# Twelve rounds of ordering by latest times in a kernel's own instruction scheduler, with new durations, a shared VectorE/GpSimd port, and other places for the last block's weight tiles

## Chip, cores and metric

The kernel runs on 1 core of one Trainium2 chip. The metric is the device time of one execution in microseconds (us). Three runs of the kernel before took 1750.62, 1752.32 and 1753.2 us; the median, 1752.32 us, is the number to beat.

## What is computed

Three stages follow each other on 4608 tokens of 512 features, all in float32:

```python
def reference(q, k, v, w_gate, w_val, w_out, w_in, w_out2):
    # attention inside chunks of 64 tokens: batch 8, heads 8, sequence 576, head size 64
    s = (q_c @ k_c.T) / 8;  a = exp(s - max(s));  a = a / (sum(a) + 1e-9)
    x = (a @ v_c)                      # 4608 x 512
    # layer 1: inner size 1536
    g = x @ w_gate
    x = (g * sigmoid(g) * (x @ w_val)) @ w_out
    # layer 2: inner size 2048
    h = x @ w_in
    return (h * sigmoid(1.702 * h)) @ w_out2
```

## The kernel before

**Tiling.** Attention works on units of 128 tokens (36 of them, `attend`, L464). Both layers work on blocks of 512 tokens (nine blocks). The weights of layer 1 are taken in two passes of six slices of the inner size, those of layer 2 in two passes of eight: passes 0 and 1 are layer 1, passes 2 and 3 are layer 2. Attention for a block is done inside pass 0, one block ahead of its use; block 0's attention has nothing to hide behind. A pass runs over all nine blocks, and in each block over its groups (three in layer 1, two in layer 2). Partial results of passes 0 and 2 go to DRAM and are added in passes 1 and 3.

**A group.** Each group multiplies two 2x2 block matrices by seven products in place of eight (`product`, L568; the inputs of the seven come from sums made beforehand, `token_combos` for the tokens and `combos` for the weights). Every float32 operand is split into a high and a low part (`split`, L244: ScalarE casts the high part, VectorE or GpSimd subtracts it from the source for the low part), and `mm3` (L248) issues three matmuls for each pair, on L249, L250 and L251. A product is 12 matmuls of 128x256 into one PSUM bank. What follows a product reads its bank: a ScalarE copy, or a VectorE addition. In layer 1 the products take turns between two banks (`ga` and `gb`, or `s` and `a`). In layer 2 all products of a group go to the one bank `ga`, some of them on top of the sum that is there (`group_gated`, L631), so a product may start only when what followed the last one has read the bank.

**Second multiplication.** Layer 1 has `second` (L622, three matmuls of 128x512 into `ya` or `yb`, here called a Y piece). Layer 2 has `last_product` (L715, six matmuls of 128x256 into `ya`, `yb`, `gb`, `s` or `a`, here a filler, since it stands between products). These pieces wait in a list, `pend`, and are taken between the products of the next group. A group of layer 2 has 7 products and 14 fillers.

**Weights.** They come from the host in packed form and are converted on the way in (`conv_part`, L323: two ScalarE and two VectorE instructions for 128x512), in pass 0 right before use for that pass, later as jobs spread over the pass before. Tiles live in rings of SBUF places: ring `w` has 21 places, ring `o` has 3. In pass 3 the first group's second weights stay in `w` for all blocks; the second group's are loaded anew in each block into the three places of `o` (in `fn` inside the main loop). A load into a place waits until the fillers that read the earlier tile are through.

**Order.** The kernel lists about six thousand operations with an engine, a duration in us, a due time (`prio`), reads and writes (`Program.op`, L76). `emit` (L99) then walks forward in time: on the engine that can start first it takes, among the operations that could start within 0.3 us (0.1 us on VectorE) of the earliest, the one with the lowest `prio`, and issues it. Durations are formulas such as `act_us`, `dve_us` and `pool_us` (L213 to L219). When data goes from another engine to TensorE, the planner allows `late` extra time: 1.2 us, or `near` where an operation names it, 1.0 us for most of layer 2 (`prog.slack`, L904). Every engine, and the DMA queue of SyncE, runs its list in the order in which it was issued, so an instruction that waits holds up all that stand behind it on its engine. 24 single matmuls with priority 9999 (L824) fill TensorE before the first product.

**End.** `o_sum` (L733) adds up the output quarters in pass 3: for the last two quarters GpSimd adds three times in a row (`yv`, `t`, `t`) to tiles loaded from DRAM, VectorE adds the last bank, and SyncE stores.

Of the kernel before, what the change touches and what calls it, by code (L numbers as in the profile page):

```python
# [9 lines left out]
F32R = mybir.dt.float32r  # L10
# [3 lines left out]
ALU = mybir.AluOpType  # L14
# [12 lines left out]
class Buf:  # L27
# [3 lines left out]
    def __init__(self, make, prev=None, before=None, whole=None):  # L31
        self.make, self.prev, self.before, self.whole = make, prev, before, whole
        self.users, self.writers, self.tile = [], [], None
# [18 lines left out]
class Ring:  # L52
    def __init__(self, pool, tag, bufs):
# [12 lines left out]
class Op:  # L66
    __slots__ = ("eng", "us", "fn", "prio", "deps", "follows", "table", "near", "n", "done_at")


class Program:  # L70


    def __init__(self):
        self.ops, self.slack = [], None

    def op(self, eng, us, fn, reads=(), writes=(), prio=0, table=None, near=None):  # L76
        o = Op()
        o.eng, o.us, o.fn, o.prio, o.table, o.near, o.n = eng, us, fn, prio, table, self.slack if near is None and eng not in ('pe', 'dma') else near, len(self.ops)
# [20 lines left out]
    def emit(self):  # L99
        waiting = {o: len(o.deps) + len(o.follows) for o in self.ops}  # L100
        after = {}
        for o in self.ops:
            for d in (*o.deps, *o.follows):
                after.setdefault(d, []).append(o)
        ready = {}
        for o in self.ops:
            o.done_at = 0.0
            if not waiting[o]:
                ready.setdefault(o.eng, []).append(o)
        free, table = {}, None  # L110
        left = len(self.ops)
        while left:
            pick = None
            for eng, todo in ready.items():
                if not todo:
                    continue
                t = free.get(eng, 0.0)
                start = [max(t, o.done_at) for o in todo]
                first = min(start)
# [5 lines left out]
            free[o.eng] = s + o.us + (1.3 if o.table and o.table != table else 0.0)  # L125
            end = free[o.eng] + (2.0 if o.eng == "dma" else 0.0)
            table = o.table or table
            o.fn()
            left -= 1
            for a in after.get(o, ()):  # L130
                if o in a.deps:
# [3 lines left out]
                    a.done_at = max(a.done_at, end + ((0.0 if a.eng == "pe" else 0.13) if a.eng == o.eng else late))  # L135
                waiting[a] -= 1
                if not waiting[a]:
                    ready.setdefault(a.eng, []).append(a)
# [3 lines left out]
def attention_two_moe_kernel(ctx: ExitStack, tc: tile.TileContext, q, k, v, wg, wv, wo, wi, wo2, out):  # L142
# [45 lines left out]
    for name, space in (("const", None), ("sb", None), ("ps", PSUM), ("dram", DRAM)):  # L188
# [5 lines left out]
    ring.update({tag: Ring(pool["ps"], tag, 1) for tag in ("ya", "yb", "ga", "gb", "s", "a")})  # L194
# [36 lines left out]
    def copy(dst, src, n, prio, eng="act", cut=lambda ap: ap, near=None):  # L231
        if eng == "act":
            op("act", act_us(n), lambda: nc.scalar.copy(out=dst.ap, in_=cut(src.ap)), [src], [dst], prio, near=near)  # L233
        elif eng == "pool":
            op("pool", pool_us(0.6 * n), lambda: nc.gpsimd.tensor_copy(dst.ap, cut(src.ap)), [src], [dst], prio)  # L235
        else:
            op("dve", dve_us(n), lambda: nc.vector.tensor_copy(dst.ap, cut(src.ap)), [src], [dst], prio)
# [39 lines left out]
    GV, YS, OS = 1.42, 0.70, 0.714  # L277
# [45 lines left out]
    def conv_part(raw, t, n, prio):  # L323
# [4 lines left out]
        op("act", act_us(n), lambda: nc.scalar.activation(  # L328
            out=t.ap, in_=raw.ap[:, :, 2], func=AF.Relu, scale=up, bias=offset.ap[:, :1]), [raw, offset], [t], prio)
        op("act", act_us(n), lambda: nc.scalar.activation(  # L330
            out=word(1).bitcast(F32), in_=raw.ap[:, :, 2], func=AF.Relu, scale=up, bias=offset.ap[:, 1:]),
           [raw, offset, t], [raw], prio)
        op("dve", dve_us(1.3 * n), lambda: nc.vector.scalar_tensor_tensor(
            out=t.ap.bitcast(I32), in0=t.ap, scalar=-4096 * up, in1=word(1).bitcast(F32), op0=ALU.add, op1=ALU.min),
           [raw, t], [t], prio)
        op("dve", dve_us(1.4 * n), lambda: nc.vector.scalar_tensor_tensor(
# [127 lines left out]
    def attend(u, prio, load_prio, bufs=None, both=None):  # L464
# [20 lines left out]
        op("pe", 1.2, lambda: blocks(s.ap, qb.ap, kb.ap), [qb, kb], [s], prio)  # L485
        m = ring["m"].new([P, H, 1])
        z = ring["z"].new([P, H, 1])
        op("dve", 0.69, lambda: nc.vector.tensor_reduce(out=m.ap, in_=heads(s.ap), axis=AX.X, op=ALU.max), [s], [m], prio)
        op("dve", 0.71, lambda: nc.vector.tensor_tensor(
            out=heads(e.ap), in0=heads(s.ap), in1=m.ap.to_broadcast([P, H, CH]), op=ALU.subtract), [s, m], [e], prio)  # L490
        op("act", act_us(512), lambda: nc.scalar.activation(out=e.ap, in_=e.ap, func=AF.Exp, scale=scale), [e], [e], prio, "exp")
        op("dve", 0.69, lambda: nc.vector.tensor_reduce(out=z.ap, in_=heads(e.ap), axis=AX.X, op=ALU.add), [e], [z], prio)
        op("dve", 0.24, lambda: nc.vector.tensor_scalar(out=z.ap, in0=z.ap, scalar1=1e-9, scalar2=None, op0=ALU.add),
           [z], [z], prio)
        op("dve", 0.2, lambda: nc.vector.reciprocal(out=z.ap, in_=z.ap), [z], [z], prio)
        op("dve", 0.71, lambda: nc.vector.tensor_tensor(
# [12 lines left out]
        op("pe", 0.75, transposes, [e, ident], [pt], prio)  # L509
        op("act", 0.59, lambda: nc.scalar.copy(out=e.ap, in_=pt.ap), [pt], [e], prio)  # L510
        o = ps() if both is None else pt
        op("pe", 1.2, lambda: blocks(o.ap, vb.ap, e.ap), [vb, e], [o], prio)
# [353 lines left out]
    for p, (layer, gs) in enumerate(passes):  # L866
        jobs = spread(p)
        for b in range(NB):
            t = start[p][b]
            xs = X.pop((p, b))  # L870
            for j, g in enumerate(gs):
# [31 lines left out]
                else:  # L903
                    prog.slack = 1.0  # L904
# [88 lines left out]
```

## Time and profile before

| what | value |
|---|---|
| median of three runs | 1752.32 us (1750.62 to 1753.2) |
| the profiled execution's own time | 1753.21 us |
| its span, first to last instruction | 1751.4 us |
| mean granted TensorE clock | 0.987 |
| TensorE matmul busy | 1704.3 us, 97% |
| VectorE, ScalarE, GpSimd busy | 1111.5, 882.3, 735.2 us |
| DMA traffic | 477.91 MB, 273 GB/s |

The profiled execution took 1.8 us more than its span. A matmul in a stream is followed by the next one well before its own shown duration ends, so busy time on TensorE overstates how full it is; what tells is the time from one matmul's start to the next one's. Waits that are listed for PE are those of a matmul, those for PEld of the weight load ahead of it.

### The profile page before, as it was taken

Reading aid. Unit: us, or ns where it says so; the run is one execution under the profiler, and the core shown is the slowest. Engines: PE = TensorE matmul, PEld = TensorE weight load, DVE = VectorE, ACT = ScalarE, POOL = GpSimd, SP = SyncE. Lnnn points to the kernel's source line nnn. Section 1 sums busy time; section 2 is a strip of 40 time slices with the busy share of each in tenths; the row PEclk is TensorE's granted clock in tenths of the full one; section 3 lists DMA queues with packets and bytes.
Section 4 is the critical chain, followed back from the end, with each engine's and each line's share of the span. In section 5 each row is a group of like instructions: output and inputs, shape, how many; then the busy total and the mean of one; then the engine's idle time right before and its main releaser. Section 6 shows DMA issues by size and latency. Waiting matters only on the chain.

```text
span 1751.4 us, 36463 instructions
## 1 busy us (share of the span) xinstructions
PE 1704.3 (97%) x14392; PEld 1617.2 (92%) x14392; DVE 1111.5 (63%) x1632; ACT 882.3 (50%) x1535; POOL 735.2 (42%) x762
## 2 busy tenths in 40 slices
PE   6889999999999999999999999999999999999998
PEld 6779989889999999999999989999999999999997
DVE  6887678767774464544445548778775555555555
ACT  5776666666763343333333446555544444444442
POOL 4665464636652145212222235656662133333333
PEclk8989999999999999999999999999999999999999
DMA  6568888887869988777778998989989977777774
GB/s 246 188 230 279 289 293 280 270 270 276 295 229 366 331 290 292 260 251 246 254 258 281 352 353 279 320 288 312 310 299 321 364 248 227 218 233 232 228 223 137
DMA packets 187323, 477.91 MB, mean 273 GB/s; under 512 B 20112, under 2 KB 47760, under 8 KB 187152
## 3 DMA queue, kind: packets, MB, share of 16 engines
q1 hardware_dynamic: 187152, 475.58, 80.5%
q8 instruction: 114, 1.87, 0.4%
q14 instruction: 57, 0.47, 0.1%
HBM read 334.46 MB, written 141.03 MB: 271 GB/s over the span
## 4 chain that ended last, share of the span: by engine, by line
PE 86%; DVE 5%; ACT 2%; issue 2%; DMA 1%; POOL 0%; POOLq 0%; ACTq 0%; DVEq 0%
PE ga L249 11%; PE ga L251 10%; PE ga L250 10%; PE yb L249 4%; PE ya L250 4%; PE ya L249 4%; PE ya L251 4%; PE yb L251 4%; PE yb L250 4%; PE gb L249 4%; PE gb L251 4%; PE gb L250 4%; PE s L249 2%; PE s L251 2%; PE s L250 2%
## 5 line engine op out<-in xcount | busy, mean ns | idle before, releaser
L249 PE MATMUL ga<-x,w 128*128 128x256 f32 x1640 | 472.9, 288 | 10.9 <-ACT u L233 3.9
L250 PE MATMUL ga<-x,w 128*128 128x256 f32 x1640 | 463.9, 283 | 3.0 <-DVE x L242 3.0
L251 PE MATMUL ga<-x,w 128*128 128x256 f32 x1640 | 464.6, 283 | 0.4 <-POOL w L242 0.4
L249 PEld LDWEIGHTS ga<-x,w 128*128 128x128 f32 x1640 | 311.7, 190 | 26.7 <-ACT u L233 9.8
L250 PEld LDWEIGHTS ga<-x,w 128*128 128x128 f32 x1640 | 311.6, 190 | 8.2 <-DVE x L242 3.3
L251 PEld LDWEIGHTS ga<-x,w 128*128 128x128 f32 x1640 | 311.5, 190 | 0.6 <-POOL w L242 0.6
L233 ACT COPY u<-ga 128x512 f32<-128x512 f32 x231 | 135.3, 586 | 254.3 <-PE ga L251 252.1
L242 DVE TENSOR_TENSOR c<-u,ga 128x512 f32<-128x512 f32 x143 | 98.2, 687 | 239.1 <-PE ga L251 229.7
L653 ACT ACTIVATE xr<-c 128x512 f32<-128x512 f32 x140 | 88.3, 631 | 135.1 <-DVE c L242 128.2
L242 DVE TENSOR_TENSOR c<-u,gb 128x512 f32<-128x512 f32 x125 | 85.4, 683 | 95.7 <-ACT u L233 68.0
L249 PE MATMUL gb<-x,w 128*128 128x256 f32 x500 | 143.4, 287 | 1.5 <-DVE c L242 1.5
L251 PE MATMUL gb<-x,w 128*128 128x256 f32 x500 | 141.8, 284 | 0.0
L250 PE MATMUL gb<-x,w 128*128 128x256 f32 x500 | 141.6, 283 | 0.0
L613 ACT ACTIVATE h<-c 128x512 f32<-128x512 f32 x108 | 67.9, 632 | 118.6 <-DVE c L242 118.0
L235 POOL CAST ws<-t 128x256 fp32r<-128x256 f32 x78 | 41.0, 526 | 193.7 <-DMA wd_b<-ws 85.5
L242 DVE TENSOR_TENSOR xr<-xr 128x512 f32<-128x512 f32 x140 | 117.4, 839 | 5.4 <-ACT xr L653 3.1
L242 POOL TENSOR_TENSOR k<-xr,q 128x512 fp32r<-128x512 f32 x24 | 37.5, 1564 | 173.8 <-ACT q L233 64.7
L242 DVE TENSOR_TENSOR hl<-h,hh 128x512 fp32r<-128x512 f32 x108 | 92.0, 872 | 17.0 <-ACT hh L233 16.8
L249 PEld LDWEIGHTS gb<-x,w 128*128 128x128 f32 x500 | 95.4, 191 | 4.3 <-DVE c L242 1.7
L242 POOL TENSOR_TENSOR u<-u 128x512 f32<-128x512 f32 x36 | 48.7, 1352 | 117.7 <-ACT u L233 117.7
L242 POOL TENSOR_TENSOR yv<-yv,e 128x512 f32<-128x512 f32 x18 | 23.2, 1288 | 177.2 <-ACT e L233 115.9
L250 PEld LDWEIGHTS gb<-x,w 128*128 128x128 f32 x500 | 95.5, 191 | 2.0
(253 smaller groups left out, 5077.0 us busy)
## 6 DMA issues: line engine op xcount, KB each, us to landing
x<-x_dram SPq DMA_DIRECT2D x189, 512.0 KB, 5.3
o<-od_b SPq DMA_DIRECT2D x126, 512.0 KB, 4.7
o<-od_a SPq DMA_DIRECT2D x102, 512.0 KB, 5.3
x_dram<-x SPq DMA_DIRECT2D x63, 512.0 KB, 4.3
wd_b<-ws SPq DMA_DIRECT2D x56, 256.0 KB, 5.0
od_b<-ws SPq DMA_DIRECT2D x56, 256.0 KB, 5.1
w<-wd_b SPq DMA_DIRECT2D x28, 512.0 KB, 6.2
raw<-in_moe_w_out SPq DMA_DIRECT2D x56, 255.8 KB, 4.8
```

The source lines that it names most:

```text
L233: op("act", act_us(n), lambda: nc.scalar.copy(out=dst.ap, in_=cut(src.ap)), [src], [dst], prio, near=near)
L235: op("pool", pool_us(0.6 * n), lambda: nc.gpsimd.tensor_copy(dst.ap, cut(src.ap)), [src], [dst], prio)
L242: lambda: e.tensor_tensor(out=dst.ap, in0=of_a(a.ap), in1=of_b(b.ap), op=by), [a, b], [dst], prio, near=near)
L249: nc.tensor.matmul(o, ah, bh, start=first, stop=False, **kind)
L250: nc.tensor.matmul(o, ah, bl, start=False, stop=False, **kind)
L251: nc.tensor.matmul(o, al, bh, start=False, stop=last, **kind)
L613: op("act", act_us(512), lambda h=h, i=i: nc.scalar.activation(out=h.ap, in_=of(0)(c[i].ap), func=AF.Silu), [c[i]], [h], prio, "silu")
L653: op("act", act_us(512), lambda: nc.scalar.activation(out=h.ap, in_=c.ap, func=AF.Gelu_apprx_sigmoid), [c], [h], prio, "gelu")
```

## The change

The change touches the planner, the durations that it is given, and one ring.

- `order` takes the place of the forward walk of `emit`. It picks by `key` in place of `prio`, with a window and a start time for each engine. Operations of GpSimd and those of VectorE that read no PSUM bank (and aren't exempt by `port=False`) share a port: the second one of two starts to work when the port is free. The switch of ScalarE's function table costs 1.28 us. A DMA costs 0.47 us of issue, and transfers stand in line at 0.865 of their nominal time. From TensorE to another engine 0.32 us are allowed (`HOP`), and 0.5 us on top (`SLACK`), or `near`, where TensorE waits for another engine.
- `dues` walks backward from the end and gives each operation its latest time. `replay` runs the list in order without slack, with a TensorE clock of two levels, and returns the end. `emit` does this twelve times, each time with keys halfway between the old key and the latest time, and issues the list with the earliest end.
- The durations are new, conversions have their own (`conv_us`), and `prog.slack = 1.0` is gone.
- In the last block of the last pass the second group's weight tiles take places of ring `w` in place of ring `o`.

The diff, cut to its core:

```diff
@@ class Ring
+        b.bank = self.pool is self.banks
@@ class Program
-        self.ops, self.slack = [], None
+    HOP = {("pe", "dve"): 0.32, ("pe", "act"): 0.32, ("pe", "dma"): 0.3}
+    WINDOW = {"pe": 0.3, "dve": 0.1, "act": 0.3, "pool": 0.3, "dma": 0.0}
+    FREE = {"pe": 1.3, "pool": 0.7, "dma": 0.7, "act": 0.0, "dve": 0.0}
+    SLACK = 0.5
+    LOAD = 1.28
+    ROUNDS = 12
...
+        o.port = eng == "pool" or eng == "dve" and port is not False and not any(a.bank for b in reads for a in b.line())
@@ def emit -> hop, order, dues, replay, emit
-                s, o = min(((s, o) for s, o in zip(start, todo) if s <= first + (0.1 if eng == "dve" else 0.3)), key=lambda x: (x[1].prio, x[1].n))
...
-                    late = (0.3, 1.2)[a.eng == "pe" and o.eng != "pe"] + (1.5 if o.eng == "dma" else 0.0)
-                    if a.near is not None and o.eng != "dma":
-                        late = a.near
+    def hop(self, d, o):
+        return 0.0 if d.eng == o.eng else self.HOP.get((d.eng, o.eng), 0.06)
+    def order(self):
...
+                t = free[eng]
+                limit = min(max(t, o.ready) for o in todo) + self.WINDOW[eng]
+                o = min((o for o in todo if o.ready <= limit), key=lambda o: (o.key, o.n))
+                s = max(t, o.ready)
...
+            if o.eng == "dma":
+                free["dma"] = s + 0.47
+                moved = max(s + 1.5, moved) + 0.865 * o.us
+                o.end = moved + 1.3
+            else:
+                if o.table and o.table != table:
+                    s, table = s + self.LOAD, o.table
+                if o.port:
+                    o.end = max(s + 0.1, port) + o.us - 0.1
+                    port = o.end - 0.1
+                else:
+                    o.end = s + o.us
+                free[o.eng] = o.end - (0.05 if o.eng != "pe" else 0.0)
...
+                    late = self.hop(o, a)
+                    if a.eng == "pe" != o.eng:
+                        late += self.SLACK if a.near is None else a.near
+                    a.ready = max(a.ready, o.end + late)
...
+    def dues(self, seq):
...
+                    t = min(t, a.due - self.hop(o, a) - (self.SLACK if a.eng == "pe" != o.eng else 0.0))
...
+            elif o.eng == "pe":
+                o.due = free = min(t, free) - o.us
+            else:
+                o.due = t - o.us
...
+    def replay(self, seq):
...
+                s = max([free[eng], *(d.end + self.hop(d, o) for d in o.deps)])
...
+    def emit(self):
...
+        for i in range(self.ROUNDS):
+            seq = self.order()
+            self.dues(seq)
+            last = self.replay(seq)
+            if best is None or last < best[0]:
+                best = last, seq
+            for o in self.ops:
+                if o.prio < 9999:
+                    o.key = (o.key + o.due) / 2
+        for o in best[1]:
             o.fn()
@@ durations (others likewise: matmul pieces, softmax steps, GV, YS, OS)
-        return (200 + n) / 1.2e3
+        return 0.23 + n / 1.385e3
+    def conv_us(n):
+        return 0.30 + n / 1.113e3
-        return (148 + n) / 0.96e3
+        return 0.15 + n / 0.966e3
-        return (128 + n) / 0.46e3
+        return 0.18 + n / 0.465e3
@@ main loop, layer 2
-                    prog.slack = 1.0
...
-                                        w = ws[n] = ring["o"].new([P, 2, 2, 256], F32R)
+                                        tag = "w" if (p, b) == (NPASS - 1, NB - 1) else "o"
+                                        w = ws[n] = ring[tag].new([P, 2, 2, 256], F32R)
```

Two places on TensorE, one on VectorE and one on the DMA queue show how instructions move. Line numbers of the change are about 119 higher.

**TensorE, a stretch of pass 3 in the steady state**, from the last matmul of one product (`ga<-x,w`) over the filler (`yb<-w,...`; `w` holds its weights, `hh` and `hl` the high and low part) to the first matmul of the next product. Before:

```order
L251 MATMUL ga<-x,w 128x256
L249 MATMUL yb<-o,h 128x256
L250 MATMUL yb<-o,h 128x256
L251 MATMUL yb<-o,h 128x256
L249 MATMUL yb<-o,h 128x256
L250 MATMUL yb<-o,h 128x256
L251 MATMUL yb<-o,h 128x256
L249 MATMUL ga<-x,w 128x256
```

And in the changed kernel, from the second of the filler matmuls that follow a product to the first matmul of the next:

```order
L369 MATMUL yb<-w,hh 128x256
L370 MATMUL yb<-w,hl 128x256
L368 MATMUL yb<-w,hh 128x256
L369 MATMUL yb<-w,hh 128x256
L370 MATMUL yb<-w,hl 128x256
L368 MATMUL yb<-w,hh 128x256
L369 MATMUL yb<-w,hh 128x256
L370 MATMUL yb<-w,hl 128x256
L368 MATMUL yb<-w,hh 128x256
L369 MATMUL yb<-w,hh 128x256
L370 MATMUL yb<-w,hl 128x256
L368 MATMUL ga<-x,w 128x256
```

Before, six filler matmuls stand between these two products; now twelve. In all of layer 2, six filler matmuls alone stand between two products 32 times before (8 in pass 2, 24 in pass 3) and 3 times now, all in pass 2. None at all, with the bank `ga` on both sides, is found 4 times before, all at the start of pass 2, and 4 times now, 2 at the start of pass 2 and 2 in the first block of pass 3. The other places have twelve or more, or another bank.

**VectorE at the start**, from the first sum of block 0's tokens (`xt<-xr`) to the low part of the first product's input (`x<-xr,x`). Rows `t<-...` are conversions of weights. Before:

```order
L242 TENSOR_TENSOR xt<-xr 128x512
L336 SCALAR_TENSOR_TENSOR t<-w,t 128x512
L242 TENSOR_TENSOR xt<-xr,xt 128x512
L530 TENSOR_TENSOR xr<-xr 128x2x256
L333 SCALAR_TENSOR_TENSOR t<-t,raw 128x256
L242 TENSOR_TENSOR xt<-xt,xr 128x512
L336 SCALAR_TENSOR_TENSOR t<-raw,t 128x256
L242 TENSOR_TENSOR x<-xr,x 128x512
```

Now:

```order
L361 TENSOR_TENSOR xt<-xr 128x512
L649 TENSOR_TENSOR xr<-xr 128x2x256
L452 SCALAR_TENSOR_TENSOR t<-t,raw 128x256
L361 TENSOR_TENSOR x<-xr,x 128x512
L455 SCALAR_TENSOR_TENSOR t<-raw,t 128x256
```

Four rows fewer stand between the tokens' first sum and the low part of the first input: a conversion of 512 columns has moved ahead of the sum, two more sums and one conversion have moved behind.

**SyncE's DMA queue at the end** of the program, with the last weight tiles `o` or `w` of pass 3 (`od_b_96` in DRAM), `yv` and `t` for the output sums. Before:

```order
L226 DMA o<-od_b_96 128x1024 x3
L229 DMA out<-yv 128x2x256
L226 DMA yv<-o_dram 128x512
L229 DMA out<-t 128x2x256 x2
L226 DMA t<-o_dram 128x512
L226 DMA o<-od_b_96 128x1024 x3
L229 DMA out<-yv 128x2x256
L226 DMA o<-od_b_96 128x1024
```

Now:

```order
L345 DMA w<-od_b_96 128x1024
L345 DMA o<-od_b_96 128x1024
L345 DMA w<-od_b_96 128x1024
L345 DMA yv<-o_dram 128x512
L345 DMA o<-od_b_96 128x1024
L345 DMA w<-od_b_96 128x1024 x2
L348 DMA out<-yv 128x2x256
L348 DMA out<-t 128x2x256
```

The last block's seven tiles go to `w`, and stand ahead of the stores `out<-yv` and the loads `yv` and `t` that they stood among.

On TensorE at the start, the first Y piece (`ya<-hh,o`) stands behind 9 products before and behind 10 now. On VectorE, six conversions stand between the gating multiplication for it (`h<-h,c`) and the first low part (`hl<-h,hh`) before, four shorter ones now. Once products have begun, a unit's transposes (L507 `a<-ident,e`) stand directly ahead of the matmuls that need their copy (L483 `a<-e,v`) once before, in block 0, and nowhere now. ScalarE loads a function table 43 times before and 51 times now; two of the eight more are among its first 125 rows.

## Rows read from the trace of the kernel before

**Rows 1.** PE waits, 0 to 131 us: for what, us in total, times, longest.

```profile
PE a L483 <- ACT e L510: 5.3, 2, 3.7
...
PE ya L250 <- DVE hl L242: 3.2, 2, 2.1
PE ga L250 <- DVE x L242: 3.0, 1, 3.0
...
PE ya L249 <- ACT hh L233: 2.3, 2, 2.0
```

**Rows 2.** Windows: busy us of five engines, PEclk, DMA share, GB/s.

```profile
34.00:48.00 14.00, 7.74 (x43) 6.97 (x39) 14.00 (x18) 11.38 (x22) 13.69 (x13) 0.51 0.50 178
```

**Rows 3.** Timeline of VectorE, 32 to 39 us: start, us, instruction.

```profile
32.26 0.68 DVE L242 TENSOR_TENSOR xt<-xr 128x512 f32<-128x512 f32 x1
...
34.60 1.21 DVE L530 TENSOR_TENSOR xr<-xr 128x512 f32<-128x512 f32 x1
35.74 0.94 DVE L333 SCALAR_TENSOR_TENSOR t<-t,raw 128x256 int32<-128x256 f32 x1
...
38.60 1.21 DVE L242 TENSOR_TENSOR x<-xr,x 128x512 fp32r<-128x512 f32 x1
```

**Rows 4.** Timeline of PE, pass 3, a product behind one filler.

```profile
1473.50 0.28 PE L251 MATMUL s<-w,xt 128*128 128x256 f32 x1
1473.81 0.39 PE L249 MATMUL ga<-x,w 128*128 128x256 f32 x1
1474.03 0.28 PE L250 MATMUL ga<-x,w 128*128 128x256 f32 x1
```

**Rows 5.** Timeline of ScalarE in the same place.

```profile
1473.17 0.59 ACT L233 COPY u<-ga 128x512 f32<-128x512 f32 x1 [1.37 <-PE ga L251]
```

**Rows 6.** Timeline of PE, pass 3, a product behind two fillers.

```profile
1476.64 0.28 PE L251 MATMUL yb<-w,hl 128*128 128x256 f32 x1
1476.77 0.28 PE L249 MATMUL ga<-x,w 128*128 128x256 f32 x1
```

**Rows 7.** Window of one block of pass 3.

```profile
1453.70:1494.45 40.75, 40.70 (x338) 40.13 (x337) 22.83 (x34) 18.44 (x32) 13.59 (x10) 1.00 0.75 231
```

**Rows 8.** Weight-load waits (PEld) of pass 3, 1390 to 1700 us.

```profile
PEld ga L249 <- ACT u L233: 3.4, 15, 0.2
PEld ga L249 <- ACT c L233: 1.1, 7, 0.2
```

**Rows 9.** Timeline of PE, start of pass 2, a product behind no filler.

```profile
1036.71 0.39 PE L249 MATMUL ga<-x,w 128*128 128x256 f32 x1 [0.68 <-ACT u L233]
```

**Rows 10.** PE waits, 1700 us to the end.

```profile
PE a L249 <- DMA o<-od_b: 2.6, 1, 2.6
PE yb L249 <- DMA o<-od_b: 0.8, 1, 0.8
PE gb L249 <- DMA o<-od_b: 0.5, 1, 0.5
```

**Rows 11.** Timeline of VectorE at the end.

```profile
1741.42 0.69 DVE L242 TENSOR_TENSOR e<-e,s 128x512 f32<-128x512 f32 x1 [0.96 <-PE s L251]
...
1746.83 0.69 DVE L242 TENSOR_TENSOR t<-t,a 128x512 f32<-128x512 f32 x1 [2.06 <-POOL t L242]
```

**Rows 12.** Timeline of ScalarE, a switch of its function table.

```profile
56.77 0.58 ACT L233 COPY xr<-a 128x512 f32<-128x512 f32 x1
57.37 1.28 ACT L613 ACT_TABLE_LOAD   x1
58.66 1.15 ACT L613 ACTIVATE h<-c 128x512 f32<-128x512 f32 x2
```

**Rows 13.** PE waits, 131 to 548 us (rest of pass 0).

```profile
PE a L507 <- DVE e L496: 3.1, 2, 2.8
```

**Rows 14.** The page, part 5: busy us, mean ns; idle before, releaser.

```profile
L242 DVE TENSOR_TENSOR c<-u,ga 128x512 f32<-128x512 f32 x143 | 98.2, 687 | 239.1 <-PE ga L251 229.7
...
L242 DVE TENSOR_TENSOR xr<-xr 128x512 f32<-128x512 f32 x140 | 117.4, 839 | 5.4 <-ACT xr L653 3.1
```

More of the change, by code (lines that the diff above doesn't have):

```diff
@@ L31, in __init__ @@
     def __init__(self, make, prev=None, before=None, whole=None):
[L32 removed]
+        self.make, self.prev, self.before, self.whole, self.bank = make, prev, before, whole, False
         self.users, self.writers, self.tile = [], [], None
@@ L97, in op @@
         return o
-    def emit(self):
-        waiting = {o: len(o.deps) + len(o.follows) for o in self.ops}
-        after = {}
+    def hop(self, d, o):
+        return 0.0 if d.eng == o.eng else self.HOP.get((d.eng, o.eng), 0.06)
+    def order(self):
+        ready = {eng: [] for eng in self.FREE}
         for o in self.ops:
[L103 to L112, printed above, removed]
+            o.ready, o.left = 0.0, len(o.deps) + len(o.follows)
+            if not o.left:
+                ready[o.eng].append(o)
+        free, table, port, moved, seq = dict(self.FREE), None, 0.0, 0.0, []
+        while len(seq) < len(self.ops):
             pick = None
@@ L124, in emit @@
             ready[o.eng].remove(o)
-            free[o.eng] = s + o.us + (1.3 if o.table and o.table != table else 0.0)
-            end = free[o.eng] + (2.0 if o.eng == "dma" else 0.0)
-            table = o.table or table
-            o.fn()
-            left -= 1
-            for a in after.get(o, ()):
-                if o in a.deps:
-                    late = (0.3, 1.2)[a.eng == "pe" and o.eng != "pe"] + (1.5 if o.eng == "dma" else 0.0)
-                    if a.near is not None and o.eng != "dma":
-                        late = a.near
[L135 to L138, printed above, removed]
+            o.begin = s
@@ new lines, in order @@
+            seq.append(o)
+            for a in o.after:
+                if o in a.deps:
+                    late = self.hop(o, a)
+                    if a.eng == "pe" != o.eng:
+                        late += self.SLACK if a.near is None else a.near
+                    a.ready = max(a.ready, o.end + late)
+                a.left -= 1
+                if not a.left:
+                    ready[a.eng].append(a)
+        return seq
+    def dues(self, seq):
+        last = max(o.end for o in seq)
+        for o in seq:
+            o.left = len(o.after)
+        heap = [(-o.end, -o.n, o) for o in seq if not o.left]
+        heapq.heapify(heap)
+        free = last
+        while heap:
+            o = heapq.heappop(heap)[2]
+            t = last
+            for a in o.after:
+                if o not in a.deps:
+                    t = min(t, a.due)
+                else:
+                    t = min(t, a.due - self.hop(o, a) - (self.SLACK if a.eng == "pe" != o.eng else 0.0))
+            if o.eng == "dma":
+                o.due = t - 2.8 - 0.865 * o.us
+            elif o.eng == "pe":
+                o.due = free = min(t, free) - o.us
+            else:
+                o.due = t - o.us
+            for d in (*o.deps, *o.follows):
+                d.left -= 1
+                if not d.left:
+                    heapq.heappush(heap, (-d.end, -d.n, d))
@@ new lines, in replay @@
+    def replay(self, seq):
+        queue = {eng: [] for eng in self.FREE}
+        for o in reversed(seq):
+            queue[o.eng].append(o)
+            o.end = None
+        free, table, port, moved = dict(self.FREE), None, 0.0, 0.0
+        busy, clock, beat = {}, 0.5, 0
+        left, last = len(seq), 0.0
+        while left:
+            pick = None
+            for eng, todo in queue.items():
+                if not todo or any(d.end is None for d in todo[-1].deps):
+                    continue
+                o = todo[-1]
+                s = max([free[eng], *(d.end + self.hop(d, o) for d in o.deps)])
+                if pick is None or s < pick[0]:
+                    pick = s, o
+            s, o = pick
+            queue[o.eng].pop()
+            left -= 1
+            us = o.us
+            if o.eng == "dma":
+                free["dma"] = s + 0.47
+                moved = max(s + 1.5, moved) + 0.865 * us
+                o.end = moved + 1.3
+                continue
+            if o.eng == "pe":
+                while beat < s // self.BEAT:
+                    share = busy.get(beat, 0.0) / self.BEAT
+                    clock = 1.0 if share > 0.85 else 0.5 if share < 0.5 else clock
+                    beat += 1
+                if clock < 1.0 and us < 3.0:
+                    us *= 1.8
+                t = s
+                while t < s + us:
+                    k = t // self.BEAT
+                    e = min(s + us, (k + 1) * self.BEAT)
+                    busy[k] = busy.get(k, 0.0) + e - t
+                    t = e + 1e-9
+            if o.table and o.table != table:
+                s, table = s + self.LOAD, o.table
+            if o.port:
+                o.end = max(s + 0.1, port) + us - 0.1
+                port = o.end - 0.1
+            else:
+                o.end = s + us
+            free[o.eng] = o.end - (0.05 if o.eng != "pe" else 0.0)
+            last = max(last, o.end)
+        return last
```

53 lines of the change are left out of this document (31 added, 22 removed).

## Prediction, made before the changed kernel ran

> **What bounds the kernel now.** I read the windows first. One block of pass 3 has TensorE busy for 40.70 of 40.75 us, while no other engine that computes is busy for more than 22.83 [rows 7]: TensorE bounds the steady state, and there only what makes TensorE pause can pay. At the start it is different. From 34 to 48 us TensorE is busy for 7.74 of 14 us, at a granted clock of 0.51, that is, mostly at 1.2 GHz, and VectorE for all 14, GpSimd for 13.69 [rows 2]. So I read PE's waits of the first 131 us next, to see who ends them [rows 1], then, since a matmul's shown duration hides short pauses, the starts of single matmuls in the steady state [rows 4, 6] beside the waits of the weight loads [rows 8], and last the waits at the end [rows 10]. TensorE's work is the same before and after, so the sum is one of pauses: which go, which stay, which come.
>
> **Short fillers in layer 2.** Matmuls of a stream start 0.12 us apart (0.13 from filler to product behind two fillers [rows 6]). Behind one filler the product's first matmul starts 0.31 us after the filler's last, and its second 0.22 us after that [rows 4]: 0.31 + 0.22 - 2 x 0.12 = 0.29 us lost. The cause is in the same place on ScalarE: the copy that frees the bank starts at 1473.17 and takes 0.59 us, to 1473.76, and the product starts at 1473.81 [rows 5], whereas the filler ended its run of starts at 1473.50. One filler is six matmuls, 0.71 us; two are 1.43 us, and cover the copy with half a microsecond to spare. A second reading: the block of [rows 7] holds 336 matmuls, 336 x 0.119 = 39.98 us, so 0.77 us are lost; three such places lie in a block, 0.26 us each. I take 0.28. In pass 3 the trace names 15 + 7 = 22 such waits [rows 8]. The order has 32 of these places before and 3 now. Gain: 29 x 0.28 = **8.1 us**. Bounds: nothing, if another engine is late at the same places, to 9.3 us (all 32 at 0.29). A product behind no filler waits longer, 0.68 us [rows 9], but there are four of these before and four now: 0.
>
> **The start, up to 131 us.** Four waits can be followed in the order.
>
> - The first product's low input. VectorE begins the tokens' first sum at 32.26 and the low part at 38.60, 6.34 us later. In the new order only the sum itself (0.68), the sum of 34.60 (1.21) and a conversion (0.94) stand ahead [rows 3]: about 2.8 us, 3.5 us less. PE's wait there is 3.0 us [rows 1], so I take 3.0.
> - The first Y pieces wait 2.3 us for high and 3.2 us for low parts [rows 1]. One product more stands ahead of them (12 x 0.12 = 1.4 us), and between gating and low part VectorE has four conversions of 256 columns where it had six, two of them of 512: about 1.5 us less by the 0.94 us of [rows 3]. I take 3.0 of the 5.5.
> - The transposes' copy: 5.3 us in two waits, the longest 3.7 [rows 1], at the one place in block 0 where the matmuls that need the copy follow directly. Now another piece lies between. I take 2.5 of the 3.7, since ScalarE's list, not only the copy, made it long.
> - The clock. 14 us at 0.51 [rows 2] cost as much as the time in which TensorE had work at half speed; with 6 to 8 us of waits gone TensorE is granted 2.4 GHz sooner. I take 2.0, between 0 and 7 (half of 14).
>
> Against this stand two more loads of ScalarE's function table, 1.28 us each [rows 12], 2.6 us if they delay what TensorE waits for, and I count them in full. Sum: 3.0 + 3.0 + 2.5 + 2.0 - 2.6 = **7.9 us**. The other waits of block 0 (weight splits on GpSimd, copies) I leave as they are: the list of splits is as long as before, and GpSimd is full there [rows 2]. Bounds: from -3, if nothing is gained and the loads delay, to 16, if all of 3.0 + 5.5 + 5.3 goes and the clock gives 2.
>
> **The rest of pass 0.** Waits listed there sum to 3.1 us [rows 13]; the six further table loads fall into time when ScalarE has room. I count 0, with 4 us either way.
>
> **The end.** The last three fillers wait 0.8, 0.5 and 2.6 us for tiles that had no free place in ring `o` [rows 10]. In `w` the tiles can be loaded a block earlier, and the waits go. But this doesn't give 3.9 us. From the seventh sum's input (1741.42) to VectorE's last addition (1746.83) lie 5.41 us, which GpSimd's three additions set: the last addition is released by GpSimd's `t`, not by the last filler [rows 11]. So the 2.6 us wait lies beside that chain, and only the 0.8 + 0.5 = 1.3 us ahead of it count, and a little for restarts: **1.5 us**, between 0 (the parts `h` and `k` become the late ones) and 3.9.
>
> **Durations, port, keys** are no instructions; they act through the order alone. Price 0 beyond what stands above.
>
> **Sum.** 8.1 + 7.9 + 1.5 = 17.5 us. The profiled execution took 1753.2 us; 1753.2 - 17.5 = 1735.7. The median of the runs is 0.9 us under that execution, so I predict **1735 us**.
>
> **Rivals.**
>
> 1. *The start only slides.* With VectorE and GpSimd full from 34 to 48 us [rows 2], a wait that is removed comes back at the next weight split: the start gives 0. For it: GpSimd's 13.69 of 14 us. Against it: TensorE's waits name VectorE and ScalarE, and order decides there. Time: 1735 + 8 = 1743 us.
> 2. *Table loads.* Eight more loads of 1.28 us [rows 12], each ahead of something that TensorE waits for: 10.3 us in place of the 2.6 counted, 1735 + 7.7 = 1743 us. Against it: in pass 0 PE's waits from 131 us on sum to 3.1 us only [rows 13], although ScalarE switches its table all through it. The Trainium skill, "ScalarE: Activation LUTs", section "What ACT_TABLE_LOAD costs", speaks against this change more strongly: it adds a drain of about 1.38 us to each load of 1.28 us, 2.66 us for each switch; an estimate by this is 8 x 2.66 = 21 us, which would leave no gain at all. The trace doesn't show such a drain: a copy ends at 57.35, the load begins at 57.37 and ends at 58.65, and the next function starts at 58.66 [rows 12].
> 3. *Two fillers aren't enough where VectorE frees the bank.* Three of the seven products of a group are followed by a VectorE addition, 0.69 us; if the addition stands behind another sum of 0.84 us [rows 14], that is 1.53 us, over the 1.43 us of two fillers. These are 3 x 36 = 108 products; if each lost 0.28 us, 30 us would come in: 1735 + 30 = 1765 us, slower. It turns the result from 63 lost products on (17.5 / 0.28). Against it: before, most products already stand behind two fillers, with the same VectorE work, and pass 3's listed waits are ScalarE's alone [rows 8].
> 4. *The start gets worse by what layer 2 gains*, about 9.5 us (one block's chain held up by a long in-order wait on ScalarE or GpSimd): 1753 us, no change.
>
> **How the numbers follow.** My forecast 0.58; rival 1 0.18, rival 2 0.06, rival 3 0.09, rival 4 0.09. A change of 0.2% (3.5 us) is about what a measurement of this kernel can tell from none. Forecast and rivals 1 and 2 are faster: 0.82. Rival 4: same, 0.09. Rival 3: slower, 0.09. The forecast's own range is 1724 (start 16, end 3.9, all fillers) to 1743. To hold 8 in 10 I go up to 1749, which takes in rivals 1 and 2, and down to 1719, which adds 4 us of the rest of pass 0.
>
> **What would show it.** Right: in pass 3 a block takes 40.0 us in place of 40.75, and the weight loads' waits for ScalarE are gone; the first product's second matmul no longer waits for VectorE, and the clock from 34 to 48 us is above 0.51; block 0's waits sum to about 8 us less; at the end no wait for `od_b`, and GpSimd's `t` still releases the last addition. Wrong: block periods at or above 40.75 us with waits for VectorE's `c` (rival 3); PE's waits in the first 131 us as long as before, under other names (rival 1); waits behind ScalarE right after a table load (rival 2).

## The result, and the profile after

The changed kernel took **1779.2 us** in the median of four runs (1772.06 to 1781.06), the kernel before 1752.76 beside it: a ratio of **1.0139 [1.0104, 1.0175]**, slower, outside the range and on the other side of the forecast. The profiled execution took 1781.06 us, its span 1779.2 us.

The page gives busy time and span first, and the chain of work that ended last in its part 4. After:

```profile
span 1779.2 us, 36540 instructions
...
PE 1704.4 (96%) x14392; PEld 1617.9 (91%) x14392; DVE 1135.2 (64%) x1632; ACT 898.5 (50%) x1543; POOL 731.5 (41%) x762
...
PE 64%; DMA 13%; POOL 8%; DVE 6%; ACT 5%; issue 3%; SPq 0%; POOLq 0%; ACTq 0%; DVEq 0%
```

The same line of part 4 for the kernel before:

```profile
PE 86%; DVE 5%; ACT 2%; issue 2%; DMA 1%; POOL 0%; POOLq 0%; ACTq 0%; DVEq 0%
```

TensorE is as busy as before (1704.4 against 1704.3 us) and does the same matmuls, but the chain that ends last now passes through transfers for 13% of the span, where it was 1%. Where that is, the windows tell. Columns: stretch, length, then busy us (instructions) of PE, PEld, DVE, ACT, POOL, granted clock, DMA share, GB/s. Before:

```profile
131.00:578.00 447.00, 443.57 (x4250) 405.61 (x4250) 317.51 (x501) 276.59 (x464) 228.45 (x270) 1.00 0.84 286
578.00:1000.00 422.00, 421.35 (x2920) 392.33 (x2919) 219.46 (x299) 148.16 (x264) 119.14 (x112) 1.00 0.83 278
1000.00:1300.00 300.00, 295.52 (x2433) 291.68 (x2432) 219.57 (x309) 169.64 (x303) 171.28 (x188) 1.00 0.90 310
1300.00:1700.00 400.00, 399.62 (x3311) 394.86 (x3310) 224.71 (x328) 179.92 (x304) 119.67 (x92) 1.00 0.79 258
```

After:

```profile
131.00:578.00 447.00, 426.75 (x4099) 386.53 (x4098) 327.92 (x506) 282.35 (x472) 263.12 (x325) 0.99 0.84 293
578.00:1000.00 422.00, 422.00 (x2931) 393.77 (x2931) 208.23 (x284) 143.12 (x245) 76.81 (x53) 1.00 0.75 259
1000.00:1300.00 300.00, 280.74 (x2223) 273.11 (x2223) 204.28 (x289) 159.09 (x281) 164.71 (x190) 0.98 0.89 305
1300.00:1700.00 400.00, 398.45 (x3344) 397.74 (x3343) 235.32 (x328) 185.29 (x311) 113.96 (x85) 1.00 0.77 254
```

Two stretches lose: the rest of pass 0 (131 to 578 us; 443.57 us busy became 426.75) and pass 2 (1000 to 1300; 295.52 became 280.74). To compare stretches that hold the same work I went by products. Pass 0 has 189, pass 1 and so on begin with the 190th, 379th and 505th, and their first matmul is in PE's timeline; from the time between two such starts I took off the matmuls that stand there, at their spacing in an undisturbed stream (0.119 us for 256 columns, 0.232 for 512, other kinds likewise). What is left is TensorE's **loss**. Its level in the first two columns depends on the spacing taken for attention's small matmuls; the differences hardly do. The column of pass 3 goes to the start of the last product.

| loss in us, one profiled execution | to the 25th product | rest of pass 0 | pass 1 | pass 2 | pass 3 |
|---|---|---|---|---|---|
| before | 54.7 | 20.1 | 2.2 | 8.3 | 7.2 |
| changed | 48.4 | 41.8 | 1.4 | 30.2 | 2.6 |
| difference | -6.3 | +21.7 | -0.8 | +21.9 | -4.6 |

The end, behind the last product, gained about 4 us more; together that is the span's difference, 27.8 us. So the gains that I priced came, nearly, and 43.6 us came in beside them, at two places that I priced at 0. PE's waits there (columns: what waits, for what, us in total, times, longest), 131 to 578 us after:

```profile
PE s L602 <- DMA k<-in_k: 4.9, 3, 2.6
PE a L602 <- DMA v<-in_v: 4.6, 3, 2.2
PE a L602 <- ACT e L629: 4.2, 6, 1.6
PE ga L368 <- ACT u L352: 3.4, 5, 1.4
```

and 1000 to 1300 us:

```profile
PE gb L368 <- DMA x<-x_dram: 2.6, 1, 2.6
...
PE yb L368 <- DMA o<-od_b: 2.4, 2, 2.0
...
PE gb L368 <- DMA o<-od_b: 2.0, 2, 1.2
```

Before, one row of 3.1 us stood in the first stretch [rows 13], and no wait for a transfer. What makes `k` late is best seen in the chain that ended last, here its pieces from 169 to 186 us (start, us, what):

```profile
169.03 0.71 POOL ws L361
169.76 7.00 DMA wd_a<-ws
176.81 0.41 POOL ws L354
177.29 1.07 POOL ws L361
178.38 0.33 SPq L348
178.80 0.38 SPq L345
179.23 5.34 DMA k<-in_k
184.57 0.14 issue
184.71 1.53 PE s L602 x32
```

A store of converted weights (`wd_a<-ws`, 256 KB) lands 7.00 us after its issue. Only then may GpSimd write the next weights into its place. The next store, at the head of SyncE's queue, waits for that (1.4 us), and behind the store in the queue stand the loads of `q` and `k`. The load of `k` takes 5.34 us, and TensorE pauses. The pause costs more than its length. PE's timeline shows the wait, and the windows ahead of it and behind it the clock:

```profile
184.71 1.53 PE L602 MATMUL s<-k,q 64*64 64x64 f32 x32 [2.61 <-DMA k<-in_k]
```

```profile
170.00:181.70 11.70, 11.70 (x139) 11.11 (x137) 11.50 (x19) 8.51 (x13) 8.74 (x10) 1.00 1.03 388
184.70:188.60 3.90, 3.89 (x44) 3.78 (x45) 1.39 (x2) 1.28 (x3) 2.33 (x5) 0.58 0.49 159
```

TensorE had 2.4 GHz up to the pause (granted clock 1.00); in the 3.90 us behind it the granted clock was 0.58, mostly 1.2 GHz, which takes, by estimate, another 3.9 x 0.42 = 1.6 us. Up to the pause the DMA engines were busy all the time, too (share 1.03, 388 GB/s): a part of the 7.00 and 5.34 us may be time in line behind other transfers, which no run tried apart.

**The suspicion.** The planner's own picture of a transfer has changed, in lines that the diff shows and I read past. In the new `order` a transfer of 256 KB lands 1.5 + 0.865 x 0.74 + 1.3 = 3.44 us after issue if no other is ahead of it in line, and its reader may start 0.06 us later (TensorE 0.56). Before, it was 0.74 + 2.0, and then 1.5 + 0.3 us up to the reader (TensorE 1.2 in place of 0.3): 4.54 and 5.44 us. The line with `+ (1.5 if o.eng == "dma" else 0.0)` is among the removed ones. The trace's list of transfers (KB each, median us from issue to landing) says what they really take, after:

```profile
wd_b<-ws SPq DMA_DIRECT2D x56, 256.0 KB, 4.3
...
k<-in_k SPq DMA_DIRECT2D x33, 256.0 KB, 4.5
v<-in_v SPq DMA_DIRECT2D x33, 256.0 KB, 4.9
```

A transfer with none ahead of it is thus planned faster than nearly all are in the median. Of 28 kinds of 256 KB only four have a median at or under 3.44 us, and these are 68 of 700 transfers.

### The profile page after: what moved, and what is told of

It is laid out like the page before. It is cut to its first block, busy times and chain, and to the rows that moved or that the text cites. A ratio compares the mean times of both kernels' runs of the same rounds, so it can differ in the third digit from the quotient of the medians.

```text
span 1779.2 us, 36540 instructions
## 1 busy us (share of the span) xinstructions
PE 1704.4 (96%) x14392; PEld 1617.9 (91%) x14392; DVE 1135.2 (64%) x1632; ACT 898.5 (50%) x1543; POOL 731.5 (41%) x762
## 4 chain that ended last, share of the span: by engine, by line
PE 64%; DMA 13%; POOL 8%; DVE 6%; ACT 5%; issue 3%; SPq 0%; POOLq 0%; ACTq 0%; DVEq 0%
PE ga L368 8%; PE ga L370 8%; PE ga L369 8%; PE ya L368 3%; PE ya L370 3%; PE ya L369 3%; PE yb L368 3%; PE yb L370 3%; PE yb L369 3%; PE gb L368 3%; PE gb L370 3%; PE gb L369 3%; DMA raw<-in_moe_w_out 2%; PE s L368 2%; PE s L370 2%
## 5 line engine op out<-in xcount | busy, mean ns | idle before, releaser
L361 DVE TENSOR_TENSOR xr<-xr 128x512 f32<-128x512 f32 x140 | 125.5, 897 | 16.5 <-ACT xr L772 12.3
L361 DVE TENSOR_TENSOR h<-h,c 128x512 f32<-128x512 f32 x108 | 90.0, 837 | 38.3 <-ACT h L732 37.1
L361 DVE TENSOR_TENSOR hl<-h,hh 128x512 fp32r<-128x512 f32 x108 | 87.9, 816 | 17.2 <-ACT hh L352 14.9
L447 ACT ACTIVATE t<-raw,offset 128x256 f32<-128x256 int16 x120 | 63.2, 527 | 70.1 <-DMA raw<-in_moe_w_out 34.2
```

Of the source, the lines that this page charges most:

```text
L361: lambda: e.tensor_tensor(out=dst.ap, in0=of_a(a.ap), in1=of_b(b.ap), op=by), [a, b], [dst], prio, near=near)
L447: op("act", conv_us(n), lambda: nc.scalar.activation(out=t.ap, in_=raw.ap[:, :, 2], func=AF.Relu, scale=up, bias=offset.ap[:, :1]), [raw, ...
```

## The experiments

**Theory A**: the plan lets transfers land too early (A1: readers of loads; A2: ring places behind stores, and the queue that a waiting store holds up). Rivals: **B**, the 0.5 us that TensorE is kept from other engines is too small; **C**, latest times as keys, or twelve rounds of them, give a worse order; and the ring edit by itself. Each ratio below is to runs of the kernel before on the same chip; the kernel before took 1752.0 to 1752.9 us there.

**e1. Landings 1.5 us later in the plan.**

```diff
-                o.end = moved + 1.3
+                o.end = moved + 2.8
...
-                o.due = t - 2.8 - 0.865 * o.us
+                o.due = t - 4.3 - 0.865 * o.us
```

> Edit: the planner lets a DMA's data land 1.5 us later than the change does (forward and backward walk). Theory A (the change plans loads to land too early: 256 KB about 3.5 us after issue, where its own profile shows medians of 4.5 us for k, 4.9 for v, 5.2 for x): the waits for k, v, x and o tiles in passes 0 and 2 go, some 15 to 20 us with what they hold up, 1760 us. Theory B (0.5 us of slack is too little for data that TensorE waits for from ScalarE and VectorE): as the change, 1775 to 1780. Theory C (keys drawn towards latest times): as the change, 1775 to 1780.

Measured: **1742.49 us**, 0.9942 [0.9927, 0.9956]: 36.7 us less than the changed kernel, and faster than before. PE's waits, 131 to 578 us:

```profile
PE a L626 <- DVE e L615: 1.8, 1, 1.8
PE a L602 <- DMA v<-in_v: 1.4, 1, 1.4
PE s L602 <- DMA k<-in_k: 0.6, 1, 0.6
```

The waits for `k` and `v` fell from 9.5 to 2.0 us, and those that name other engines fell with them, from 10.4 to 2.4; the loss in the rest of pass 0 fell from 41.8 to 18.2. A stands. The plan now has 5.0 us from issue to reader (TensorE 5.5), close to the 4.54 and 5.44 of the plan before. `replay`, which picks among the rounds, keeps 1.3 us here and in every other run of the changed kernel.

**e2. 1.2 us in place of 0.5 between another engine and TensorE.**

```diff
-    SLACK = 0.5
+    SLACK = 1.2
```

> Edit: SLACK 1.2 us in place of 0.5, as the kernel before allowed where TensorE waits. Theory B: the waits for ScalarE's copies and VectorE's sums in passes 0 and 2 go, 10 to 15 us, 1765 us; most places in pass 3 keep two fillers. Theory A: waits for DMA get shorter too, since they end at TensorE, but x, v and conversions are not helped: 1770. Theory C: 1775 to 1780.

Measured: 1782.85 us, 1.0190 [1.0158, 1.0223], no better than the changed kernel. B falls: the loss in pass 2 stays (30.4), and the rest of pass 0 too (39.4).

**e3. One round in place of twelve.**

```diff
-    ROUNDS = 12
+    ROUNDS = 1
```

> Edit: one round in place of twelve, so the order goes by the due times written in the program, with the new durations and port. Theory C: the loss of passes 0 and 2 goes, 1750 to 1755 us, and pass 3 keeps its gain. Theories A and B: the loss stays, 1775 to 1785.

Measured: 1793.22 us, 1.0230 [1.0215, 1.0246]. With one round the keys are the old due times, so C falls: with these landings, keys from latest times and their rounds help, by some 14 us.

**e4. The kernel before, with the ring edit alone.**

```diff
-                                        w = ws[n] = ring["o"].new([P, 2, 2, 256], F32R)
+                                        tag = "w" if (p, b) == (NPASS - 1, NB - 1) else "o"
+                                        w = ws[n] = ring[tag].new([P, 2, 2, 256], F32R)
```

> Edit: the kernel before with nothing but the last block's weight tiles in ring w. All theories: the waits for od_b at the end go, the chain of three GpSimd additions stays; 1 to 3 us faster than before, 1750 us. If the new ring were to cost something earlier, 1753 or more.

Measured: 1750.6 us (10 runs), 0.9992 [0.9982, 1.0001]. It is worth 0.08%, some 1.4 us, with zero just inside the interval. The loss is not from here.

**e5 and e6. Later landings for loads alone, and for stores alone.**

```diff
-                o.end = moved + 1.3
+                o.end = moved + 1.3 + (1.5 if o.kind == "load" else 0.0)
...
-                o.due = t - 2.8 - 0.865 * o.us
+                o.due = t - 2.8 - (1.5 if o.kind == "load" else 0.0) - 0.865 * o.us
```

(The lines that tell each transfer whether it is a load or a store are left out. In e6 `"store"` stands for `"load"`.)

> Edit: only loads land 1.5 us later in the plan, stores as in the change. Theory A1 (what hurts is that readers of k, v, x, o tiles and of raw weights are planned before the data is there): nearly all of the 37 us that both brought, 1745 to 1755 us. Theory A2 (what hurts is that a store's place in the ring is planned free too early, so GpSimd waits for the store of ws, and the stores behind it hold up the DMA queue with the loads in it): little, 1770 us.

> Edit: only stores end 1.5 us later in the plan, loads as in the change. Theory A1: little, 1770 us. Theory A2: most of the 37 us, 1745 to 1755 us, and waits of the DMA queue for GpSimd's ws well under 100 us in the rest of pass 0.

Measured: loads 1761.8 us, 1.0056 [1.0041, 1.0071]; stores 1757.35 (10 runs), 1.0028 [1.0012, 1.0044]. They take off 17.4 and 21.9 us, in sum 39.3 against 36.7 for both: two causes of like size that overlap little, as far as the scatter of e6 (1751.5 to 1765.3 us) lets one say. Neither came down to the 1745 to 1755 us that was expected if it were the whole. By the count of losses, loads take 9.4 us off the rest of pass 0 and 11.3 off pass 2, stores 10.4 and 3.6 (e6's trace is of its slowest execution, 1765.33 us). SyncE's own waits tell the two apart. The largest row, 131 to 578 us, in the kernel before and in the changed kernel:

```profile
SPq L229 <- POOL ws L242: 42.1, 36, 3.8
```

```profile
SPq L348 <- POOL ws L361: 100.5, 75, 4.6
```

in e5 and in e6:

```profile
SPq L348 <- POOL ws L361: 106.6, 73, 4.0
```

```profile
SPq L348 <- POOL ws L361: 50.5, 42, 5.5
```

Of the two, only the later stores take the queue's waiting for GpSimd away: with them the plan knows when a ring place comes free, and no longer puts a store at the head of the queue early.

**e7. 1.0 us between an engine's end and the transfer that waits for it; landings as in the change.**

```diff
+                    if a.eng == "dma" != o.eng:
+                        late += 1.0
```

> Edit: the plan allows 1.0 us more before a DMA that waits for an engine (stores of fresh results, loads into places just freed); landing times as in the change. Theory A1: loads are issued later still relative to their readers in the plan, but the plan knows it: near the change, 1770 to 1785. Theory D (the queue is held up because each store is put at the very moment its source should be ready, and loads stand behind it): waits of the queue for ws fall, k and v land in time, 1750 to 1760.

Measured: 1760.95 us, 1.0052 [1.0037, 1.0067]: 18.2 us less. The same row of SyncE falls to 78.9 us in 61 waits. The held-up queue is a real part of A, since no landing was touched here.

**e9. Landings 0.8 us later.**

```diff
-                o.end = moved + 1.3
+                o.end = moved + 2.1
...
-                o.due = t - 2.8 - 0.865 * o.us
+                o.due = t - 3.6 - 0.865 * o.us
```

> Edit: loads and stores land 0.8 us later in the plan, in place of 1.5. Theory A as a dose: about half of the 37 us, 1755 to 1765 us. If 0.8 us already covers what the trace shows as the median (4.3 to 4.9 us against 3.5 planned): as with 1.5, 1742 to 1746.

Measured: 1752.56 us (10 runs), 1.0000 [0.9989, 1.0012], between the two and a little better than the 1755 to 1765 us expected of half the dose.

**e11. The other way: landings 0.8 us earlier.** It is the control for the case that any other order would have come out faster, whatever its landings.

```diff
-                o.end = moved + 1.3
+                o.end = moved + 0.5
...
-                o.due = t - 2.8 - 0.865 * o.us
+                o.due = t - 2 - 0.865 * o.us
```

> Only the plan's landing of a transfer is changed, to 0.8 us earlier than in the changed kernel (about 2.7 us after issue for 256 KB in place of 3.5), with the due times to match. Theory A (the plan lets transfers land too early): later by 0.8 us had taken 26.6 us away, so earlier by 0.8 adds some 20 us, about 1800 us; TensorE's waits for k, v and x between 131 and 548 us get more. If the times of these orders scatter by chance: about 1780 or below.

Measured: **1811.93 us**, 1.0326 [1.0304, 1.0347], 32.7 us more than the changed kernel, where some 20 were expected. Four points on one line of edits, -0.8, 0, 0.8 and 1.5 us, give 1811.9, 1779.2, 1752.6 and 1742.5 us.

**e12. The kernel before, without its 1.5 us.**

```diff
-                    late = (0.3, 1.2)[a.eng == "pe" and o.eng != "pe"] + (1.5 if o.eng == "dma" else 0.0)
+                    late = (0.3, 1.2)[a.eng == "pe" and o.eng != "pe"]
```

> The kernel before, with only the 1.5 us taken out that its planner adds between a transfer's landing and its reader; its durations, keys and single round stay. Theory A: the old order loses what the changed one lost from the same cause, part of 20 us since 0.74 and 2.0 us stay in its landing, so about 1765 us (1757 to 1775), with more waits of TensorE for k, v and x. If the allowance matters only together with the new durations or keys: 1752, as before.

Measured: **1775.46 us**, 1.0133 [1.0099, 1.0167]. This one removed term, with the old durations, keys and single round, makes the kernel before as slow as the changed one. I had expected TensorE to wait longer for `k` and `v`; it doesn't (one wait for `k`, 0.2 us). SyncE's waits for `ws` rise from 42.1 to 62.6 us, and TensorE waits one step further on: VectorE and TensorE, 131 to 578 us:

```profile
DVE yv L237 <- DMA y_dram<-yv: 8.3, 7, 2.4
```

```profile
PE yb L249 <- DVE yv L237: 7.0, 6, 2.3
```

The tile `yv`, which carries a Y piece to DRAM, is still being stored when VectorE is to copy the next piece into it, and so the bank `yb` stays full.

**e13 and e14. Can it be pushed further?** Landings 2.0 us later (e13):

```diff
-                o.end = moved + 1.3
+                o.end = moved + 3.3
...
-                o.due = t - 2.8 - 0.865 * o.us
+                o.due = t - 4.8 - 0.865 * o.us
```

and the edit of e1 with 0.5 us at the head of the queue (e14):

```diff
-                o.end = moved + 1.3
+                o.end = moved + 2.8
...
+                    if a.eng == "dma" != o.eng:
+                        late += 0.5
...
-                o.due = t - 2.8 - 0.865 * o.us
+                o.due = t - 4.3 - 0.865 * o.us
```

> The changed kernel with landings 2.0 us later in the plan (1.5 in the fastest run so far, 1742.5 us). Theory A: the loads' allowance (about 5.5 us for 256 KB) is now past the medians of 4.5 to 5.2 us, so little is left to gain: 1738 to 1744 us. If the plan is now too slow for its ring places, products get later: 1746 or more.

> The changed kernel with landings 1.5 us later in the plan and 0.5 us kept between an engine's end and the transfer that waits for it at the head of the queue. Theory A with the queue's part (1.0 us there alone had taken 18 us off): the two partly cover the same waits, so 1736 to 1742 us. If the later landing has already taken all of it: 1742 to 1745 us.

Measured: 1743.18 us, 0.9943 [0.9928, 0.9958], and **1739.43 us**, 0.9923 [0.9904, 0.9942]. Past 1.5 us nothing more is gained. e14 is the fastest kernel measured, though its lead over e1 (3 us) is within the intervals. Part 4 of the page, by engine, for e11, e12 and e14:

```profile
PE 60%; DMA 17%; DVE 7%; ACT 6%; POOL 5%; issue 4%; SPq 1%; POOLq 0%; DVEq 0%; ACTq 0%
```

```profile
PE 71%; DMA 10%; DVE 8%; ACT 3%; issue 3%; POOL 2%; SPq 0%; POOLq 0%; DVEq 0%; ACTq 0%
```

```profile
PE 81%; DVE 5%; POOL 4%; DMA 3%; issue 3%; ACT 2%; POOLq 0%; SPq 0%; DVEq 0%; ACTq 0%
```

| loss in us | to the 25th product | rest of pass 0 | pass 1 | pass 2 | pass 3 | median run |
|---|---|---|---|---|---|---|
| e11, 0.8 earlier | 49.5 | 55.3 | 6.1 | 31.0 | 5.2 | 1811.9 |
| changed | 48.4 | 41.8 | 1.4 | 30.2 | 2.6 | 1779.2 |
| e9, 0.8 later | 44.1 | 31.7 | 1.2 | 15.2 | 2.7 | 1752.6 |
| e1, 1.5 later | 46.3 | 18.2 | 0.7 | 17.8 | 2.7 | 1742.5 |
| e14, and the queue | 45.7 | 17.5 | 1.1 | 12.4 | 6.0 | 1739.4 |
| e12, before without 1.5 | 51.4 | 32.9 | 2.5 | 16.5 | 6.7 | 1775.5 |
| before | 54.7 | 20.1 | 2.2 | 8.3 | 7.2 | 1752.8 |

Each row is one profiled execution, and not always one near the median: it took 1805.2 us in e11 and 1771.1 in e12. The allowance acts in the two places where the changed kernel lost, pass 0 and pass 2. Pass 2 loses 12.4 us even in e14, against 8.3 before; what holds that rest wasn't tried. No run has the new durations or the shared port alone either, so what they give or cost by themselves is open.

## Why the prediction was wrong

**The step that failed** is the line "Durations, port, keys are no instructions; they act through the order alone. Price 0 beyond what stands above", and with it "The rest of pass 0: I count 0, with 4 us either way". Acting through the order alone was right; that this costs nothing was not. I followed the order in four places at the start and in pass 3, and priced the rest by the waits of the kernel before, which are small because the old plan kept 4.5 to 5.4 us from issue to reader (e12: without 1.5 us of it, 12.8 us come in there and 8.2 in pass 2). The term measured +21.7 us in pass 0 and +21.9 us in pass 2, and e1 takes 36 of these 43.6 us back with the landing alone. The price couldn't be read from a wait of before, but the sign could: most 256 KB transfers of before have landing medians of 4 to 5.4 us (607 of 700), and the new plan's 3.44 us is under them.

**The rivals.** None of the four was this one. Rivals 1 and 4 put the trouble at the start, where the time got better in sum, though rival 1's mechanism is there at one place (below). Rival 2 (eight more table loads): e1 still has four more than before, 47 against 43, and yet loses less than before in the rest of pass 0 (18.2 against 20.1 us). Rival 3, the slower one, fails by the steady state below.

**Short fillers: right.** From 1450 to 1700 us, in fifths, TensorE starts 422 or 423 matmuls in 50 us. One fifth after, and the same before:

```profile
1500.00:1550.00 50.00, 50.00 (x422) 50.00 (x422) 34.36 (x45) 22.62 (x38) 18.87 (x14) 1.00 0.76 246
```

```profile
1500.00:1550.00 50.00, 49.95 (x417) 49.38 (x416) 29.26 (x42) 22.43 (x38) 16.23 (x12) 1.00 0.75 229
```

Over all five it is 2113 against 2073, so the 336 matmuls of a block take 39.75 us after and 40.52 before: 0.77 us less, as forecast (40.75 to 40.0). The 22 waits of weight loads for ScalarE [rows 8] are one, of 0.9 us, and another of 0.2; one of 1.1 us for VectorE's `c`, rival 3's sign, stands beside them, in the pass's first block. Pass 3 as a whole gained 4.6 us, where 24 of the 29 counted places would give 6.7.

**The start: about the right size, in part by luck.** 7.9 us were forecast, 6.3 came. The Y pieces' 5.5 us are gone, where I had taken 3.0. The first product's wait for its low part fell from 3.0 [rows 1] to 0.99 us, but the next product now waits 3.63 us for GpSimd's low part and a third one 2.73 for VectorE's: this wait has slid, as rival 1 said, and grown, to 7.35 us. The transposes' copy, for which I took 2.5, takes as long as ever. All listed waits to 131 us sum to 26.9 us, against 29.4 before, and not to 8 less. PE's timeline after, and its waits to 131 us:

```profile
37.96 0.58 PE L369 MATMUL ga<-x,w 128*128 128x256 f32 x1 [0.99 <-DVE x L361]
...
44.52 0.58 PE L369 MATMUL gb<-x,w 128*128 128x256 f32 x1 [3.63 <-POOL x L361]
...
50.18 0.58 PE L369 MATMUL ga<-x,w 128*128 128x256 f32 x1 [2.73 <-DVE x L361]
```

```profile
PE a L602 <- ACT e L629: 5.0, 2, 3.9
```

The clock gave nothing: 0.54 from 34 to 48 us, against 0.51 [rows 2], but 0.83 from 48 to 80, against 0.95; over the 131 us it is 0.87 both times.

**The end: the waits for `od_b` are gone as forecast** [rows 10], and 4 us came in place of 1.5, in the whole change; alone, the edit gave some 1.4 (e4). That GpSimd's `t` would still release the last addition was wrong: VectorE's three last additions now follow each other, the first of them released by GpSimd's `yv`:

```profile
1773.23 0.69 DVE L361 TENSOR_TENSOR e<-e,yb 128x512 f32<-128x512 f32 x1 [0.66 <-POOL yv L361]
1773.84 0.68 DVE L361 TENSOR_TENSOR yv<-yv,yb 128x512 f32<-128x512 f32 x1
1774.46 0.69 DVE L361 TENSOR_TENSOR t<-t,a 128x512 f32<-128x512 f32 x1
```

With the landing put right, e1 and e14 stand 10 and 13.5 us under the kernel before, where 17.5 were forecast. By the losses e1 gains 8.4 us to the 25th product (7.9 priced), 4.5 in pass 3 (6.7) and some 4 at the end (1.5), and gives 9.5 back in pass 2, where I had counted no loss. That only shows that the priced terms fit in sum; what is left in pass 2 is open.

## What to carry to other kernels

Where a planner sets the order, its cost model is part of the kernel: compare each number that it assumes with the median on the page, removed slack first, and price a number that falls below the median as a loss wherever the engine has no cover. A plan that is too early on transfers pays twice with in-order queues: the reader waits, and a store that reaches the head of the queue early holds up loads that could have run. To find such a cause, move the one number in both directions, and also take it out of the old kernel; here the time answered in all three, which leaves little room for chance, though the wait that showed it wasn't the same one each time.

## What was not expected of the hardware

The time from issue to landing spreads far more within a run than between plans. For the 33 loads of `k`, trace rows (least, median, longest) show 2.9, 4.5 and 9.0 us in the changed kernel and 3.3, 4.8 and 8.4 in e1, at a mean of 269 and 275 GB/s. The medians aren't quite the same for every plan: 4.3 us in e11, 5.0 in e9, 5.4 in e14.

The Trainium skill, "DMA: Bandwidth & Descriptors", section "Anatomy of one DMA — SWDGE (gpsimd) path", gives a fit of 2.0 us plus the bytes by 436 GB/s for one transfer; an estimate by it for 256 KB is 2.6 us, which would have called the new plan's 3.44 us generous. The fit is for transfers issued from GpSimd, these are SyncE's, and the measured medians of 4.3 to 4.9 us decide.

A wait of 2.61 us cost TensorE, by the estimate above, about 4.2 us, since the granted clock was 0.58 for 3.90 us behind it. In the rest of pass 0 the listed waits rose by 16.8 us (3.1 to 19.9), the loss by 21.7. How much of the difference is the clock, and how much short pauses that no row names, was not measured apart.
